# Fixed accumulator banks, a new order of the weights' splits, and expert 0's last chunk by column pairs, in an attention and mixture-of-experts kernel

## The chip, the cores and the metric

The kernel runs on one core of a Trainium2 chip. The time is the device time of one execution in microseconds; the median of several executions counts. Everything is computed in float32, where each matrix product is split into a high and a low part so that the tensor engine can take it in three passes.

## The reference

```python
attn = softmax(mask(q @ k.T / sqrt(64)))        # 8 batches, 8 heads, 576 positions, window of 64
x = (attn @ v) as rows [4608, 512]
noisy = x @ w_gate + log1p(exp(x @ w_noise)) * noise      # 8 experts
top2, weights = two best experts of each row, softmax over the two
for e in range(8):
    for k in range(2):
        m = top2[:, k] == e
        h = np.maximum(x[m] @ w1[e], 0.0)       # 512 -> 1024
        out[m] += weight[m] * (h @ w2[e])       # 1024 -> 512
```

## The kernel before, in words

**Stages.** Up to about 225 us the kernel computes attention and routes each row to two experts; the rows then lie in DRAM as xrows. After that it walks over a work list of chunks (e, c): expert 0 has three chunks (384, 384 and 448 rows), each of experts 1 to 7 has two (576 and 640 rows). A chunk is tiles of 128 rows, the 576 one with a fifth tile of 64.

**A chunk.** Its tokens are gathered and turned (transposed) ahead, beside the chunk before. Then PE runs the first layer (`up`) and the second (`down`).
- `gather` (L670): `whole` (L675, POOL) brings a tile's rows in by an indirect DMA into a buffer xg, of which there are four, which the outputs of the second layer use too. `turn_out` (L687) and four `turn_in` (L692), both on SP's queue, send them through DRAM so that they land as xc in blocks. `gate_of` (L679) copies the gate weight.
- `turn`: for each tile DVE transposes 32 x 32 blocks (`f`, L737, two instructions), then `g` makes the sums that the first layer's scheme wants and splits them into a high part xh (ACT, L749 and L755) and a low part xl (DVE, L751 and L756).
- `up`: for experts 1 to 7 the first layer is done by seven half-size products per group of columns g (0 to 3) in place of eight (L841 to L843 are the three passes). Product 2 opens a group in bank y, products 5 and 3 go to bank v, the others to a ring of three banks z. ACT copies (L867) or writes the relu (L853), DVE adds (L872) and makes the low part (L857). For expert 0 `up_first` runs the plain first layer, one column block f after the other.
- `down`: the second layer of a chunk by tiles. A tile takes 24 matmuls (16 for the 64-row tile), then ACT evicts it with the gate (L995; L997 and DVE's L998 and L999 for the 64-row tile) and POOL adds it into the output by an indirect DMA (`add_rows`, L917). The first tiles are interleaved with the first layer's last products.

**Banks.** `BANKS["d"]` is d0, d1 and y. `down` takes a tile's bank from the ring (L975), which runs on from chunk to chunk, so that every third tile is in y, also where the next chunk's first product opens in y.

**Weights.** `load_w2` (L218, SP) brings 2 MB of an expert's second weights into ws; `load_w1` (L214) the next expert's first weights into the same place. Each is split into a high part (ACT, L242) and a low part (DVE, L234, which `lag` puts one item later). The first weights also need POOL's sums of columns (L264): `split_w1` gives lists of items, for each column group g its `raw` parts, its `sums`, and its `mixed` parts, which are made of the sums. The second weights' load is issued when the last `mixed` part is read, since it goes to the same buffer.

**Order.** There is no scheduler: each engine takes its instructions as the program writes them. `spread(main, total, *parts)` (L77) runs the generator of matmuls and puts side work between its steps: a part (a, b, items) is laid out evenly from the fraction a to the fraction b of the `total` steps. The main loop (L1115 on) says where the gathers, the turn and the splits stand in the first and second layer of each chunk.

Of the kernel before, what the change touches and what calls it, by code (L numbers as in the profile page):

```python
# [22 lines left out]
KD, KF = DM // 128, F // 128  # L23
# [64 lines left out]
def tile_kernel(ctx, tc, qT, kT, vx, vT, wgx, noise, w1, w2, out):  # L88
# [115 lines left out]
    w2s = ws.rearrange("p (f d) -> p f d", f=KF)  # L204
# [5 lines left out]
    W2 = {}  # L210
# [17 lines left out]
    def lag(items, eng=nc.vector):  # L228
        todo = [None]

        def low_part():
            if todo[0]:
                x, h, l = todo[0]
                eng.tensor_tensor(l, x, h.bitcast(F32), op=OP.subtract)  # L234
            todo[0] = None

        def step(it):
            if callable(it):
                return lambda: (low_part(), it())

            def f():
                nc.scalar.activation(it[1], it[0], AF.Copy)  # L242
                low_part()
                todo[0] = it
            return f
        return [step(it) for it in items] + [low_part]

    def split_w1(ahead=False, add=nc.gpsimd, eng=nc.vector):
        def cols(g):
            return (w1s[:, :, x * 512 + g * 128:x * 512 + g * 128 + 128] for x in range(2))  # L250

        def parts(g, a, n, src):
            return (src, *(x.rearrange("p a k f -> p (a k) f")[:, 2 * a:2 * a + n, g * 128:g * 128 + 128]
                           for x in (WH, WL)))

        def raw(g):
            u, v = cols(g)
            return [parts(g, 0, 4, u), parts(g, 2, 2, v[:, 2:4])]

        def sums(g):  # L260
            u, v = cols(g)
            todo = ((v[:, 2:4], v[:, 0:2], v[:, 2:4], OP.add), (v[:, 0:2], v[:, 0:2], u[:, 0:2], OP.subtract),
                    (u[:, 0:2], v[:, 2:4], u[:, 0:2], OP.subtract), (u[:, 2:4], u[:, 2:4], u[:, 0:2], OP.subtract))
            return [lambda: [add.tensor_tensor(o, a, b, op=op) for o, a, b, op in todo]]  # L264

        def mixed(g):
            u, v = cols(g)
            return [parts(g, 5, 4, v), parts(g, 3, 4, u)]
        if ahead:
            return [lag([x for g in range(4) for x in raw(g) + sums(g)], eng), lag([x for g in range(4) for x in mixed(g)], eng)]  # L270
        a, b, c, d = (raw(0) + sums(0), raw(1) + sums(1) + mixed(0), raw(2) + sums(2) + mixed(1),
                      raw(3) + sums(3) + mixed(2) + mixed(3))
        return [lag(x, eng) for x in (a, b, c, d)]

    def split_w2():
        return lag([(w2s[:, f], W2["h"][:, f], W2["l"][:, f]) for f in range(KF)])


    VG = idle[:, 0:256].rearrange("p (n c) -> p n c", n=1)
# [494 lines left out]
    EXB, BANKS = {}, {}  # L774
# [8 lines left out]
    def up_first(c):  # L783
        e, n = 0, FIRST[c]
        main = n // 128 * 128
        tail = n - main
        HH[e, c] = [], [], []
        xh, xl = XH.pop((e, c)), XL.pop((e, c))
        for f in range(KF):
            if c == 0 and f < 4:  # L790
                hid = [x[:, f] for x in spare] + [None]
            else:
                if f == (0 if c else 4):
                    hb = EXB["p"].tile([128, 2, KF, 2 * HALF], F32R, name="hb")
                hid = [hb[:, 0, f, :384], hb[:, 1, f, :384],
                       hb[:, 0, f, 384:384 + 2 * tail].rearrange("p (s t) -> p s t", s=2) if tail else None]
            for a, b in zip(HH[e, c], hid):
                a.append(b)
            p = bank()
            fs = slice(f * 128, (f + 1) * 128)  # L800
            for k in range(KD):
                nc.tensor.matmul(p[:, :n], lhsT=w1h[:, k, fs], rhs=xh[:, k, :n], start=(k == 0), stop=False)
                nc.tensor.matmul(p[:, :n], lhsT=w1h[:, k, fs], rhs=xl[:, k, :n], start=False, stop=False)
                nc.tensor.matmul(p[:, :n], lhsT=w1l[:, k, fs], rhs=xh[:, k, :n], start=False, stop=(k == KD - 1))
                if k < KD - 1:
                    yield
            h, l, t = (x[f] for x in HH[e, c])
            nc.scalar.activation(h, p[:, :main], AF.Relu)
            nc.vector.scalar_tensor_tensor(l, p[:, :main], 0.0, h.bitcast(F32), op0=OP.max, op1=OP.subtract)
            if tail:  # L810
                nc.scalar.activation(t[:, 0], p[:, main:n], AF.Relu)
                nc.vector.scalar_tensor_tensor(t[:, 1], p[:, main:n], 0.0, t[:, 0].bitcast(F32),
                                               op0=OP.max, op1=OP.subtract)
            yield
# [3 lines left out]
    def ring(name):  # L818
        turns[name] += 1
        return BANKS[name][turns[name] % len(BANKS[name])]  # L820
# [135 lines left out]
    def down(e, c):  # L956
        if e == 0:
            yield from down_first(c)
            return
        wt = GW[e, c]  # L960
        hb = HH.pop((e, c))
        w2h, w2l = W2["h"], W2["l"]
        order = (0, 4, 1, 5, 2, 6, 3, 7)
        size = dict(tiles(e, c))
        steps = [(0, 0, 4), None, (0, 4, 6), (1, 0, 2), None, (1, 2, 6), (0, 6, 8), (1, 6, 8)]
        steps += [(q, 0, 8) for q in size if q > 1]
        P_ = {}
        for s in steps:
            if not s:
                yield from late.pop(0)  # L970
                continue
            q, i0, i1 = s
            m = size[q]
            if i0 == 0:
                P_[q] = ring("d")  # L975
            p = P_[q]
            for i in range(i0, i1):
                f = order[i]
                a, b = dict(start=(i == 0), stop=False), dict(start=False, stop=(i == KF - 1))
                if m == 128:  # L980
                    h, l = (hb[:, x, f, q * 128:q * 128 + 128] for x in range(2))
                    nc.tensor.matmul(p, lhsT=h, rhs=w2h[:, f, :], **a)  # L982
                    nc.tensor.matmul(p, lhsT=h, rhs=w2l[:, f, :], start=False, stop=False)  # L983
                    nc.tensor.matmul(p, lhsT=l, rhs=w2h[:, f, :], **b)  # L984
                else:
                    t = hb[:, 0, f, q * 128:q * 128 + 2 * m]
                    nc.tensor.matmul(p, lhsT=t, rhs=w2h[:, f, :], **a)
                    nc.tensor.matmul(p, lhsT=t, rhs=w2l[:, f, :], **b)
                if i < KF - 1:
                    yield  # L990
            if i1 < KF:
                continue
            y = exa.tile([128, XW], F32, name="xg", bufs=XB)[:, :DM]
            if m == 128:
                nc.scalar.activation(y, p, AF.Copy, scale=wt[:, q:q + 1])  # L995
            else:
                nc.scalar.activation(y[:m], p[m:2 * m], AF.Copy)  # L997
                nc.vector.tensor_tensor(y[:m], y[:m], p[:m], op=OP.add)  # L998
                nc.vector.tensor_scalar(y[:m], y[:m], wt[:m, q:q + 1], None, op0=OP.mult)  # L999
            add_rows(e, c, q, m, y)  # L1000
            yield
# [112 lines left out]
    for n, (e, c) in enumerate(work):  # L1114
# [3 lines left out]
        if n == 0:  # L1118
            for w in split_w2():
                side += [lambda: (drain(3), drain_slots(1))] * 2 + [w]  # L1120

            def catch_up():
                while (0, 1, 2) not in XG:
                    drain(1)
                    drain_slots(1)
        elif n == 1:
            pending.append(count())
            side += [lambda: (drain(6), drain_slots(1))] * 12
            side += [settle, lambda: drain_slots(10 ** 6), lambda: [x() for x in first_list(2)], lambda: None]
        elif c == 0:  # L1130
            parts.append((0.45, 0.95, split_w2()))
        if nxt and n:
            side += gather(*nxt) + [lambda: None] * 2
        if last and nxt:
            nextw = split_w1(e == 0)
            parts += [(0.55, 0.75, nextw[0]), (0.8, 1.0, nextw[1])] if e else [(0.1, 1.0, nextw[0])]
        parts.append((0.0, 1.0, side))
        if n == 0:
            parts.append((0.0, 0.8, [zero_out] * ZUP))
# [2 lines left out]
        total = KF * len(tiles(e, c)) + (4 if e else 0)  # L1142
        free = 12.5 / total
        if e == 0:
            parts = [(0.7, 1.0, side) if nxt[0] == 0 else (0.05, 0.9, side)]
            if last:
                parts.append((0.0, 0.8, nextw[1]))
        else:
            if c == 0:
                load_w1(e + 1)  # L1150
            parts = [(free, 0.86, side)]
            if last and nxt:
                parts.append((free, 0.9, nextw[2] + nextw[3]))
        if n == 1:
            load_w1(1)
            parts.append((0.0, 0.6, list(other_lists())))
# [125 lines left out]
```

## Time and profile before

| | |
|---|---|
| median of three executions | 1087.65 us (1087.3, 1087.65, 1090.16) |
| the profiled execution | 1086.88 us, span 1085.2 us |
| mean granted clock of TensorE | 0.969 |
| PE busy | 996.1 us, 92% |
| PE's weight loads busy | 888.8 us, 82% |
| DVE busy | 709.2 us, 65% |
| ACT busy | 521.6 us, 48% |
| POOL busy | 436.7 us, 40% |

The profiled execution is longer than its span by 1.7 us, which lie before and after what the profiler records. PE is the matrix engine, DVE the vector engine, ACT the scalar engine, POOL the general one, SP the engine that only issues DMAs here. A share is an average over stages; where PE stands still for another engine is seen only in the waits and the timelines.

### The profile page before, as it was taken

What the parts mean: (1) busy time and instruction counts of PE and PEld (TensorE: products, weight loads), DVE (VectorE), ACT (ScalarE), POOL (GpSimd) and SP (SyncE); (2) the same over time, 40 slices, a digit from 0 to 9 for tenths busy, and PEclk for the clock granted to TensorE, in tenths of its full rate; (3) what the DMA queues carried; (4) which work ended last, traced back from release to release, by engine and by line L of the source; (5) the groups of instructions that cost most, each with busy time, mean ns of one, the idle gap of its engine ahead of it and who ended that gap; (6) DMA issues with size and microseconds to landing.
All of it is one profiled execution on the core that took longest, in us unless ns stands there. A gap on an engine that the chain in (4) does not pass through costs nothing.

```text
span 1085.2 us, 22040 instructions
## 1 busy us (share of the span) xinstructions
PE 996.1 (92%) x8433; PEld 888.8 (82%) x8433; DVE 709.2 (65%) x1692; ACT 521.6 (48%) x1305; POOL 436.7 (40%) x577
## 2 busy tenths in 40 slices
PE   9887778879998999899989999998999998999995
PEld 8776777769787898889887979897989787978894
DVE  5688878583267667666776676668666756675630
ACT  4885665422245454535453445344544543554430
POOL 4436536332354154416432543255234614362202
PEclk9998997989998999999999999999999999999998
DMA  9987887783346653675267527653845485437303
GB/s 334 358 269 225 253 273 222 254 263 87 69 103 185 161 133 47 194 165 137 40 200 157 141 30 219 142 138 45 243 109 131 73 232 109 115 63 210 45 2 51
DMA packets 107235, 168.94 MB, mean 156 GB/s; under 512 B 13360, under 2 KB 57648, under 8 KB 105328
## 3 DMA queue, kind: packets, MB, share of 16 engines
q1 hardware_dynamic: 89968, 126.96, 38.2%
q0 software_dynamic: 17152, 40.48, 20.5%
q8 instruction: 68, 1.11, 0.4%
q14 instruction: 47, 0.39, 0.1%
HBM read 110.08 MB, written 57.32 MB: 154 GB/s over the span
## 4 chain that ended last, share of the span: by engine, by line
PE 56%; DVE 21%; DMA 9%; ACT 7%; issue 3%; POOL 3%; SPq 1%; POOLq 0%; DVEq 0%; ACTq 0%
PE ps_z L841 5%; PE ps_z L842 5%; PE ps_z L843 5%; PE ps_d L983 4%; PE ps_d L982 4%; PE ps_d L984 4%; PE ps_v L841 3%; PE ps_v L842 3%; PE ps_v L843 2%; PE ps_y L984 2%; PE ps_y L982 2%; PE ps_y L983 2%; DMA ws<-in_w_dram 2%; DVE xl L751 2%; DVE WL L234 2%
## 5 line engine op out<-in xcount | busy, mean ns | idle before, releaser
L917 POOL DMA_INDIRECT out_dram<-xg,los x70 | 114.7, 1638 | 264.9 <-ACT xg L995 232.9
L853 ACT ACTIVATE hb<-tq 128x288 fp32r<-128x288 f32 (+1 forms) x168 | 76.2, 459 | 147.8 <-DVE tq L872 147.5
L841 PE MATMUL ps_z<-xh,WH 128*128 128x288 f32 (+1 forms) x448 | 138.3, 309 | 0.0
L842 PE MATMUL ps_z<-xl,WH 128*128 128x288 f32 (+1 forms) x448 | 136.4, 305 | 0.0
L843 PE MATMUL ps_z<-xh,WL 128*128 128x288 f32 (+1 forms) x448 | 136.3, 304 | 0.0
L872 DVE TENSOR_TENSOR tq<-ps_z,tq 128x288 f32<-128x288 f32 (+1 forms) x168 | 78.3, 471 | 82.9 <-PE ps_z L843 82.2
L264 POOL TENSOR_TENSOR ws<-ws 128x256 f32<-128x256 f32 x112 | 94.4, 843 | 90.7 <-ACT WH L242 68.5
L983 PE MATMUL ps_d<-w2l,hb 128*128 128x512 f32 x328 | 127.8, 390 | 0.0
L982 PE MATMUL ps_d<-w2h,hb 128*128 128x512 f32 x328 | 127.8, 390 | 0.0
L984 PE MATMUL ps_d<-w2h,hb 128*128 128x512 f32 x328 | 127.7, 389 | 0.0
L857 DVE SCALAR_TENSOR_TENSOR hb<-tq,hb 128x320 fp32r<-128x320 f32 (+2 forms) x168 | 82.3, 493 | 41.0 <-ACT hb L853 37.2
L675 POOL DMA_INDIRECT xg<-xrows,lxs x70 | 72.9, 1041 | 84.9 <-DMA xs<-xg 33.1
L755 ACT ACTIVATE xh<-tq 128x512 fp32r<-128x512 f32 (+1 forms) x70 | 42.8, 611 | 101.1 <-DVE tq L753 101.1
L841 PEld LDWEIGHTS ps_z<-xh,WH 128*128 128x128 f32 x448 | 85.6, 191 | 2.8
L842 PEld LDWEIGHTS ps_z<-xl,WH 128*128 128x128 f32 x448 | 85.5, 191 | 1.1
L843 PEld LDWEIGHTS ps_z<-xh,WL 128*128 128x128 f32 x448 | 85.4, 191 | 0.0
L756 DVE TENSOR_TENSOR xl<-tq,xh 128x512 fp32r<-128x512 f32 (+1 forms) x70 | 46.6, 666 | 47.4 <-ACT xh L755 47.4
L234 DVE TENSOR_TENSOR WL<-ws,WH 128x512 fp32r<-128x512 f32 x112 | 74.7, 676 | 4.2 <-ACT WH L242 4.2
L841 PE MATMUL ps_v<-xh,WH 128*128 128x288 f32 (+1 forms) x224 | 70.7, 316 | 5.9 <-ACT tq L867 5.9
L341 POOL TENSOR_TENSOR t<-t,mx 128x512 f32<-128x512 f32 x36 | 38.0, 1055 | 93.7 <-DVE mx L340 73.1
L395 ACT ACTIVATE x<-ps_o,r 128x80 f32<-128x80 f32 x288 | 66.8, 347 | 14.4 <-DVE r L387 14.2
L984 PEld LDWEIGHTS ps_d<-w2h,hb 128*128 128x128 f32 x328 | 61.6, 188 | 13.0
(248 smaller groups left out, 2590.8 us busy)
## 6 DMA issues: line engine op xcount, KB each, us to landing
ws<-in_w_dram SPq DMA_DIRECT2D x14, 2048.0 KB, 10.3
xs<-xg SPq DMA_DIRECT2D x63, 256.0 KB, 3.5
vw<-in_vx_dram SPq DMA_DIRECT2D x36, 272.0 KB, 4.8
out_dram<-zero SPq DMA_DIRECT2D x38, 256.0 KB, 3.7
qc<-in_qT_dram SPq DMA_DIRECT2D x36, 256.0 KB, 5.0
KW<-in_kT_dram SPq DMA_DIRECT2D x36, 256.0 KB, 4.5
vt<-in_vT_dram SPq DMA_DIRECT2D x36, 256.0 KB, 4.2
xrows<-x SPq DMA_DIRECT2D x36, 256.0 KB, 4.4
```

The source lines that it names most:

```text
L234: eng.tensor_tensor(l, x, h.bitcast(F32), op=OP.subtract)
L264: return [lambda: [add.tensor_tensor(o, a, b, op=op) for o, a, b, op in todo]]
L841: nc.tensor.matmul(p[:, :n], lhsT=WH[:, a, k, w], rhs=xh[:, b, k, :n], start=first and k == 0, stop=False, **free)
L842: nc.tensor.matmul(p[:, :n], lhsT=WH[:, a, k, w], rhs=xl[:, b, k, :n], start=False, stop=False, **free)
L843: nc.tensor.matmul(p[:, :n], lhsT=WL[:, a, k, w], rhs=xh[:, b, k, :n], start=False, stop=(k == 1), **free)
L853: nc.scalar.activation(hh[:, f, a:b], src, AF.Relu)
L857: nc.vector.scalar_tensor_tensor(hl[:, f, a:m], src[:, :m - a], 0.0, hh[:, f, a:m].bitcast(F32), op0=OP.max, op1=OP.subtract)
L872: nc.vector.tensor_tensor(t, a[:, :n], t, op=OP.add)
L917: s = nc.gpsimd.indirect_dma_start(out=out[:(2 + seen.get((e, c), NT)) * 128], out_offset=bass.IndirectOffsetOnAxis(ap=LT[e, c][1][q][:m], ...
L982: nc.tensor.matmul(p, lhsT=h, rhs=w2h[:, f, :], **a)
L983: nc.tensor.matmul(p, lhsT=h, rhs=w2l[:, f, :], start=False, stop=False)
L984: nc.tensor.matmul(p, lhsT=l, rhs=w2h[:, f, :], **b)
```

## The change

Five edits:
1. `down` (experts 1 to 7): tile 0 has bank y, tiles 1 to 4 have d0, d1, d0, d1, in every chunk.
2. `split_w1`: the lists for the second layer of a last chunk. Before: raw(2), sums(2), mixed(1) and then raw(3), sums(3), mixed(2), mixed(3), one list behind the other. Now: raw(2), sums(2), raw(3), sums(3), mixed(1), mixed(2), mixed(3).
3. `split_w2` stands from 0.6 to 1.0 of a first chunk's first layer, where it stood from 0.45 to 0.95, and goes in the order in which `down` takes the blocks.
4. The turn's items end at 0.82 of the second layer (0.86 before), for expert 0 at 0.8 (0.9).
5. Expert 0's last chunk: `up_first` goes through its column blocks in the order 0, 4, 1, 5, 2, 6, 3, 7, and expert 1's first weights are split in eight lists, of which seven stand in the first layer and only mixed(3) in the second, up to 0.4 (before: one list of raw and sums in the first layer, one of all mixed in the second up to 0.8).

```diff
         if ahead:
-            return [lag([x for g in range(4) for x in raw(g) + sums(g)], eng), lag([x for g in range(4) for x in mixed(g)], eng)]
-        a, b, c, d = (raw(0) + sums(0), raw(1) + sums(1) + mixed(0), raw(2) + sums(2) + mixed(1),
-                      raw(3) + sums(3) + mixed(2) + mixed(3))
-        return [lag(x, eng) for x in (a, b, c, d)]
+            return [lag(raw(g) + sums(g), eng) for g in range(4)] + [lag(mixed(g), eng) for g in range(4)]
+        a, b, c = (raw(0) + sums(0), raw(1) + sums(1) + mixed(0),
+                   raw(2) + sums(2) + raw(3) + sums(3) + mixed(1) + mixed(2) + mixed(3))
+        return [lag(x, eng) for x in (a, b, c)]
 
     def split_w2():
-        return lag([(w2s[:, f], W2["h"][:, f], W2["l"][:, f]) for f in range(KF)])
+        return lag([(w2s[:, f], W2["h"][:, f], W2["l"][:, f]) for f in (0, 4, 1, 5, 2, 6, 3, 7)])
...
-        HH[e, c] = [], [], []
+        HH[e, c] = [None] * KF, [None] * KF, [None] * KF
...
-        for f in range(KF):
+        for f in (0, 4, 1, 5, 2, 6, 3, 7) if tail else range(KF):
...
-                a.append(b)
+                a[f] = b
...
             if i0 == 0:
-                P_[q] = ring("d")
+                P_[q] = BANKS["d"][2 if q == 0 else 1 - q % 2]
...
         elif c == 0:
-            parts.append((0.45, 0.95, split_w2()))
+            parts.append((0.6, 1.0, split_w2()))
...
             nextw = split_w1(e == 0)
-            parts += [(0.55, 0.75, nextw[0]), (0.8, 1.0, nextw[1])] if e else [(0.1, 1.0, nextw[0])]
+            parts += ([(0.55, 0.75, nextw[0]), (0.8, 1.0, nextw[1])] if e else
+                      [(a, b, nextw[q]) for q, a, b in ((0, 0.02, 0.12), (1, 0.14, 0.3), (2, 0.33, 0.5), (4, 0.34, 0.5),
+                                                       (3, 0.55, 0.75), (5, 0.56, 0.75), (6, 0.8, 1.0))])
...
         if e == 0:
-            parts = [(0.7, 1.0, side) if nxt[0] == 0 else (0.05, 0.9, side)]
+            parts = [(0.7, 1.0, side) if nxt[0] == 0 else (0.05, 0.8, side)]
             if last:
-                parts.append((0.0, 0.8, nextw[1]))
+                parts.append((0.0, 0.4, nextw[7]))
         else:
             if c == 0:
                 load_w1(e + 1)
-            parts = [(free, 0.86, side)]
+            parts = [(free, 0.82, side)]
             if last and nxt:
-                parts.append((free, 0.9, nextw[2] + nextw[3]))
+                parts.append((free, 0.9, nextw[2]))
```

The order on ACT at the end of expert 2's second layer, last chunk (L995 evicts an output tile, L242 makes a high part of weights, L749 and L755 copy turned tokens, L867 belongs to the next chunk's first layer). Before:

```order
L995 ACTIVATE xg<-ps_d_3967,wg 128x512
L242 ACTIVATE WH<-ws 128x4x128
L749 ACTIVATE xh<-tq 128x6x64
L755 ACTIVATE xh<-tq 128x8x64
L242 ACTIVATE WH<-ws 128x4x128 x2
L995 ACTIVATE xg<-ps_y_3972,wg 128x512
L749 ACTIVATE xh<-tq 128x6x32
L755 ACTIVATE xh<-tq 128x8x32
L242 ACTIVATE WH<-ws 128x4x128
L995 ACTIVATE xg<-ps_d_3966,wg 128x512
L867 ACTIVATE tq<-ps_y_3972 128x288
```

Now:

```order
L995 ACTIVATE xg<-ps_d_3967,wg 128x512
L242 ACTIVATE WH<-ws 128x4x128
L749 ACTIVATE xh<-tq 128x6x64
L755 ACTIVATE xh<-tq 128x8x64
L242 ACTIVATE WH<-ws 128x4x128 x3
L749 ACTIVATE xh<-tq 128x6x32
L755 ACTIVATE xh<-tq 128x8x32
L995 ACTIVATE xg<-ps_d_3966,wg 128x512
L242 ACTIVATE WH<-ws 128x4x128
L995 ACTIVATE xg<-ps_d_3967,wg 128x512
L867 ACTIVATE tq<-ps_y_3972 128x288
```

The last tile of the turn (the two copies of 32 columns) has moved ahead of the fourth tile's eviction, and neither of the last two evictions reads the bank that L867 reads.

POOL in the first layer of expert 0's last chunk (L264 are the column sums, L675 the gathers for expert 1, L679 the gate weights). Before:

```order
L675 DMA xg<-xrows,lxs 128x528 x4
L264 TENSOR_TENSOR ws<-ws 128x2x128 x4
L679 COPY wg<-xg 128x1
L675 DMA xg<-xrows,lxs 64x528
L264 TENSOR_TENSOR ws<-ws 128x2x128 x4
L679 COPY wg<-xg 128x1 x2
L264 TENSOR_TENSOR ws<-ws 128x2x128 x4
```

Now:

```order
L675 DMA xg<-xrows,lxs 128x528 x2
L264 TENSOR_TENSOR ws<-ws 128x2x128 x4
L675 DMA xg<-xrows,lxs 128x528 x2
L264 TENSOR_TENSOR ws<-ws 128x2x128 x4
L679 COPY wg<-xg 128x1
L675 DMA xg<-xrows,lxs 64x528
L264 TENSOR_TENSOR ws<-ws 128x2x128 x4
```

Two groups of sums now stand ahead of the fifth gather, where one did.

## Rows read from the trace of the kernel before

**Rows 1.** PE's waits, 225 us to the end (what waited <- releaser: total us, times, longest)
```profile
PE ps_y L841 <- ACT xh L749: 9.8, 5, 4.7
PE ps_y L841 <- ACT xg L995: 7.7, 2, 3.8
```

**Rows 2.** timeline of PE: first-layer products (start us, length us, [idle before, releaser])
```profile
334.89 0.61 PE L841 MATMUL ps_y<-xh,WH 128*128 128x288 f32 x1 [4.75 <-ACT xh L749]
...
441.05 0.40 PE L841 MATMUL ps_y<-xh,WH 128*128 128x288 f32 x1 [3.83 <-ACT xg L995]
...
490.66 0.30 PE L841 MATMUL ps_y<-xh,WH 128*128 128x320 f32 x1
...
559.72 0.40 PE L841 MATMUL ps_v<-xh,WH 128*128 128x288 f32 x1 [1.56 <-ACT tq L867]
...
597.46 0.41 PE L841 MATMUL ps_y<-xh,WH 128*128 128x320 f32 x1 [1.54 <-DVE xg L998]
...
915.20 0.42 PE L841 MATMUL ps_y<-xh,WH 128*128 128x320 f32 x1 [2.75 <-DVE xg L998]
```

**Rows 3.** windows of six us from such starts (length, PE busy, granted clock, DMA share, GB/s)
```profile
440.00:446.00 6.00, 4.95 (x25) 0.72 0.89 205
...
597.00:603.00 6.00, 5.54 (x37) 1.00 0.35 58
```

**Rows 4.** timeline of SP's queue: loads of second weights (L218) and first turn_in (L692)
```profile
334.11 0.35 SPq L218 DMA_DIRECT2D ws<-in_w_dram  x1
...
355.21 0.32 SPq L692 DMA_DIRECT2D xc<-xs  x1
...
441.59 0.35 SPq L218 DMA_DIRECT2D ws<-in_w_dram  x1
...
463.27 0.32 SPq L692 DMA_DIRECT2D xc<-xs  x1
...
547.26 0.35 SPq L218 DMA_DIRECT2D ws<-in_w_dram  x1
...
654.05 0.35 SPq L218 DMA_DIRECT2D ws<-in_w_dram  x1
...
758.26 0.35 SPq L218 DMA_DIRECT2D ws<-in_w_dram  x1
...
777.95 0.32 SPq L692 DMA_DIRECT2D xc<-xs  x1
...
863.90 0.35 SPq L218 DMA_DIRECT2D ws<-in_w_dram  x1
...
973.33 0.35 SPq L218 DMA_DIRECT2D ws<-in_w_dram  x1
```

**Rows 5.** timeline of DVE: first transposes of tiles in the turn (L737)
```profile
315.59 0.45 DVE L737 STREAM_TRANSPOSE tq<-xc 128x256 f32<-128x256 f32 x1 [3.77 <-DMA xc<-xs]
...
320.18 0.44 DVE L737 STREAM_TRANSPOSE tq<-xc 128x256 f32<-128x256 f32 x1
...
472.28 0.45 DVE L737 STREAM_TRANSPOSE tq<-xc 128x256 f32<-128x256 f32 x1 [0.48 <-DMA xc<-xs]
...
577.12 0.45 DVE L737 STREAM_TRANSPOSE tq<-xc 128x256 f32<-128x256 f32 x1 [0.22 <-DVE hb L857]
...
788.38 0.43 DVE L737 STREAM_TRANSPOSE tq<-xc 128x256 f32<-128x256 f32 x1
...
895.14 0.45 DVE L737 STREAM_TRANSPOSE tq<-xc 128x256 f32<-128x256 f32 x1 [1.70 <-DMA xc<-xs]
...
899.01 0.45 DVE L737 STREAM_TRANSPOSE tq<-xc 128x256 f32<-128x256 f32 x1
```

**Rows 6.** timeline of POOL: a group of sums (L264), and expert 0's last whole scatter-add
```profile
297.69 3.51 POOL L264 TENSOR_TENSOR ws<-ws 128x256 f32<-128x256 f32 x4 [0.88 <-ACT WH L242]
...
333.56 1.91 POOL L917 DMA_INDIRECT out_dram<-xg,lo  x1 [6.55 <-ACT xg L941]
```

**Rows 7.** DMA issues: the loads of whole weights (KB each, median us to landing)
```profile
ws<-in_w_dram SPq DMA_DIRECT2D x14, 2048.0 KB, 10.3
```

## The prediction

> **What bounds the kernel now.** Read the table of PE's waits from 225 us on first: in the expert part only a few rows count. The product that opens a chunk (bank y, L841) waited five times for the turned tokens, 9.8 us, and twice for an eviction, 7.7 us [rows 1]. Then go to PE's timeline for their places [rows 2]: 4.75 us at 334.89 (expert 1), 3.83 at 441.05 (expert 2; expert 5 has its like), 1.54 at 597.46 and 2.75 at 915.20 (second chunks of experts 3 and 6, on DVE's eviction of a 64-row tile). The other four waits for tokens are (9.8 - 4.75) / 4 = 1.26 each. A fourth kind stands inside a first layer: 1.56 at 559.72, a product whose bank waits for an ACT copy that stands behind the split of the second weights; experts 3, 6 and 7 have it.
>
> A wait can cost more than itself. The windows [rows 3] show PE's granted clock at 0.72 in the six microseconds after the wait of 3.83, and after that of 2.75 alike, which is part 2.4 GHz and part 1.2 GHz: 6 x 0.28 = 1.68 us of work lost. After the wait of 1.54 it stayed 1.00. After the waits of 1.26 it fell once in four.
>
> But PE's waits are the end of a loop, and the queues show what closes it. SP issues the load of an expert's second weights (L218) as soon as DVE has split the last of the first weights. Only afterwards do the last scatter-adds and the gathers for the next chunk get through, and SP's first turn_in (L692) follows 463.27 - 441.59 = 21.68 us after the load in expert 2 [rows 4]. The tokens land 9.0 us later, and DVE starts to turn them at 472.28 [rows 5], 30.69 after the load. From there to the next load it is 547.26 - 472.28 = 74.98 us: five tiles turned, a first and a second layer, the next turn, the next split. Loops last 105.67 (441.59 to 547.26), 106.79 (to 654.05) and, the longest, 109.43 (863.90 to 973.33). I read this as a chain: load, scatter-add, gather, turn, first layer, second layer, split, load. In expert 2 the turn starts 0.48 us after DVE went idle for these tokens, so there the chain holds, although PE idled 3.83 at the chunk before. That idle time was cover.
>
> **The change, part by part.** The sum is made against the profiled execution, 1086.88 us (span 1085.2), 0.77 below the median of 1087.65.
>
> *Fixed banks.* Tile 0 goes to y and the last tile to a d bank. So y is free when the next chunk opens, and the waits on evictions (3.83 twice, 1.54, 2.75) have no cause left. What it is worth depends on the chain. Expert 2's and expert 5's 3.83 lie ahead of a chain that was late anyway: removed, the same time appears at the second chunk, where turned tokens are needed. The arithmetic: the last tile's first copy ends 4 x 3.87 (895.14 to 899.01 [rows 5]) + two transposes of 0.45 + 0.5 = 16.9 after the turn starts, thus 30.7 + 16.9 = 47.6 after the load. PE opened that chunk at 490.66 [rows 2] without a wait, 49.1 after the load, and without the 3.83 and the 1.68 that followed it would come at 43.6. So 4 us of waiting return there, and I count nothing for expert 2 on this account. Expert 3's 1.54 and expert 6's 2.75 lie after the turn, on the path: turn to load took 76.93 in expert 3 (577.12 to 654.05) and 78.19 in expert 6 (895.14 to 973.33) against 74.98, so 1.95 and 3.21 go.
>
> *Two banks where three ran on.* Tile 4 now needs tile 2's eviction. Tile 3 covers it; a few tenths at most, under the chain: 0.
>
> *Turn earlier (0.82), fewer mixed splits in front.* In the second layer one split on DVE (the 0.72 by which a tile with splits, 4.59, is longer than one without, 3.87; both below) fewer stands before the third tile. The turn of the next first chunk, for which PE waits 1.26, comes 0.4 earlier (0 to 0.7). In six loops: -2.4 (-4.2 to 0).
>
> *Second weights split later.* They leave the place where the ACT copy waited behind them; 1.56 goes in experts 3, 6 and 7, but in front of the late tokens, so it is cover like expert 2's. One thing remains: in expert 5 the turn at 788.38 began 10.43 after its turn_in (777.95), where 9.01 would do (463.27 to 472.28); earlier work on DVE held it. 1.42 goes, and 0.54 of its 75.52 to the load: -1.96.
>
> Gains: expert 1, 2 and 4 nothing but the 0.4 each; 3: 1.95; 5: 1.96; 6: 3.21; and 2.4: **-9.5**.
>
> *What it costs.* In the second layer of a last chunk the eviction of the fourth tile (L995) now stands on ACT behind the turn's last copy (L755); before it stood ahead of that tile's two copies, as the order shown with the change has it. Its scatter-add is therefore issued just as the load starts, and moves its 256 KB beside the load's 2048 KB, which take 10.3 us [rows 7]. The nearest row is expert 1's: a whole tile's scatter-add was issued at 333.56 [rows 6], the load at 334.11, the turn_in at 355.21, 21.10 after it, against 21.68 in expert 2 and 19.69 in expert 5 (758.26 to 777.95), mean 20.69 [rows 4]. I take +0.4 in six loops, **+2.4**. Lower bound 0, since the gathers wait for buffers either way; upper 1.3 a loop, an eighth of 10.3.
>
> The Trainium skill, "DMA: Bandwidth & Descriptors", Queues, rings and completion order, says that each engine takes turns between the queues that have work for it, packet by packet. By it the load would be stretched by all of the scatter-add's bytes, an estimate of 1.3 us a loop, and the forecast would read 5.4 us later; expert 1's row shows less.
>
> *Half clock at second chunks.* PE will wait there now, 4 us in expert 2, about as long in 6, and near none to 2 in the others. By the windows a wait of 2.75 or more costs 1.68; I take two of the six: **+3.4** (0 to 8.4). The half clock of expert 2 and 5 after the eviction falls away, but lies in the cover.
>
> *Expert 0's last chunk.* Its groups' sums and mixed splits move into the first layer, so the second layer has one list left instead of two. On POOL one more group of sums, four operations of together 3.51 us [rows 6], stands before the last gather, which had 0.88 us idle ahead of it: tokens 2.6 later than 315.59, where DVE waited 3.77 for them [rows 5]. In return, the turn has fewer splits between its tiles: 3.87 a tile where none stands there, for the 4.59 from 315.59 to 320.18, three tiles long: -2.2. Net **+0.4** (-2.2 to +2.6).
>
> Sum: -9.5 + 2.4 + 3.4 + 0.4 = -3.3, thus 1083.6 for the profiled execution and **1084.3** for the median, 0.3% less. With the bounds the case has a range of 1078 to 1091.
>
> **Rivals.** *The waits simply vanish.* If the chain is looser than I read it (the gathers' time shrinks when PE runs earlier, because scatter-adds and buffers come earlier as well), all that PE waits is gained: 7.7 + 1.54 + 2.75 of evictions, 3 x 1.56 before products, about 2.5 of the waits for tokens, 3 x 1.68 of half clock: 24 us, 1063.4. For it: nothing in rows 4 says that 21.68 could not shrink (in expert 5 it is 19.69). Against it: nothing in the change moves the gathers ahead of the load, and with 30.69 after every load DVE stood waiting. 0.18.
>
> *Slower: the scatter-add in the load's shadow.* The eviction behind the turn puts the fourth tile's scatter-add beside the load in every loop; the gather that reuses its buffer waits for it, and 1.3 us a loop go into the chain, 6 x 1.3 = 7.8. PE then waits at second chunks by enough for the half clock in five loops, 8.4. -9.5 + 7.8 + 8.4 + 0.4 = +7.1: **1094.8**. It decides from 0.9 us a loop with four half clocks (5.4 + 6.7 + 0.4 > 9.5 + 3). For it: the order on ACT is plain, and the half clock follows each long wait. Against it: 21.10 in expert 1. 0.24.
>
> *It does nothing:* the gains are cover throughout and costs small. This lies inside my own case, whose range holds both signs.
>
> **Chances.** My case 0.58, vanish 0.18, slower 0.24. Some 0.3% (3.3 us) is what a measurement of this kernel can tell from no change: 1084.4 to 1090.9. My forecast lies on that border: of its 0.58, 0.26 falls below, 0.31 inside, 0.01 above. Faster 0.44, same 0.31, slower 0.25. The range reaches to 1070 and 1095, which leaves out most of the first rival and the worse half of the second, some 0.2.
>
> **What would show it.** Right: no wait of a y product for an eviction in the waits; waits of 1 to 4 us on xh or xl at second chunks (about 486 and 806); load to turn still 29 to 31 us; turn to load 74.5 to 75 in all loops; no wait near 560. The first rival: load to turn falls to 27 or less. The second: turn_in 22 or more after the load, and granted clock 0.72 after five second chunks' openings. I am wrong if PE still waits on y, if loops differ by over 2 us, or if expert 1 starts later than 337.

## The result, and the profile after

The changed kernel takes 1099.61 us in the median of eight executions (1093.98 to 1109.98), the kernel before 1087.71 (1086.43 to 1090.35) beside it: ratio 1.0106, 95% interval 1.0066 to 1.0147. It is slower by some 1.1%, where I had forecast 0.3% less, and it lies beyond my range. In these eight executions it also spreads four times as far, 16.0 us against 3.9; that this belongs to the change is not shown, since the kernel before spread over 14.2 us in 29 later executions.

The profiled execution took 1101.77 us (span 1100.0). Waits of PE from 225 us on, what waited <- releaser, total, times, longest (answers to [rows 1]):

```profile
PE ps_y L841 <- ACT xh L749: 11.6, 7, 5.1
PE ps_d L982 <- ACT xg L995: 5.7, 6, 1.6
...
PE ps_d L987 <- ACT xg L995: 2.7, 3, 1.1
```

The waits of a chunk's first product for an eviction are gone, as the change means it, and so are the waits of v products near 560. New are waits on ps_d: tile 4 for tile 2's eviction, and nothing of the kind stood in the table before. The waits for tokens went from five to seven, and moved: before, they stood at first chunks; now, but for expert 1's, at second ones, where PE's timeline has, for the second chunk of expert 2:

```profile
497.78 0.41 PE L841 MATMUL ps_y<-xh,WH 128*128 128x320 f32 x1 [1.46 <-ACT xh L749]
```

Half speed follows. Windows (length, PE busy, granted clock, DMA share, GB/s) behind the openings of the second chunks of experts 2, 3, 4 and 6, as against [rows 3]:

```profile
498.00:506.00 8.00, 7.54 (x28) 0.58 0.25 33
608.00:614.00 6.00, 6.00 (x30) 0.72 0.36 46
714.00:720.00 6.00, 5.84 (x28) 0.72 0.30 40
929.00:935.00 6.00, 5.77 (x29) 0.72 0.34 44
```

Four of seven, each with a part of the stretch at 1.2 GHz; I had counted two. The first costs 8 x 0.42 = 3.4 us, the others 1.7 each, together 8.4. The trace before has four such stretches as well, at other places (from 441, 653, 759 and 916 on, granted clock 0.72 over six us each, together 6.7). In sum that is 1.7 us more than before.

The queue of SP shows where the time went. Load of the second weights (L218) and first turn_in (L692), experts 2, 3 and 6, as against [rows 4]:

```profile
448.35 0.35 SPq L218 DMA_DIRECT2D ws<-in_w_dram  x1
...
471.88 0.32 SPq L692 DMA_DIRECT2D xc<-xs  x1
...
558.47 0.35 SPq L218 DMA_DIRECT2D ws<-in_w_dram  x1
...
579.89 0.32 SPq L692 DMA_DIRECT2D xc<-xs  x1
...
877.41 0.35 SPq L218 DMA_DIRECT2D ws<-in_w_dram  x1
...
900.96 0.32 SPq L692 DMA_DIRECT2D xc<-xs  x1
```

From load to turn_in it is 23.53, 21.42 and 23.55 us. Over experts 2 to 7 the mean is 22.48; in the trace before it was 20.78. DVE, at the first tile of the turn, waits as the end of this (answers to [rows 5]):

```profile
480.90 0.77 DVE L737 STREAM_TRANSPOSE tq<-xc 128x256 f32<-128x256 f32 x2 [4.98 <-DMA xc<-xs]
```

**Where the 14.8 us of the two spans lie.** Up to the start of expert 1's second turn 5.90, of which 3.74 stand already at 225 us, in code that the change does not touch (that stage ended between 225.5 and 234.0 in the 14 traces of this study, whatever the kernel). From that turn to expert 2's load 0.86. In the five loops from expert 2's load to expert 7's 6.23: 5.48 from load to turn, 0.75 from turn to load. Behind the last load 1.81. The medians differ by 11.9; without the 3.74 the traces differ by 11.1.

Laid against the forecast: from load to turn, experts 2 to 7, I had +1.0 (2.4 less expert 5's 1.42), and it is 5.48 and 1.81, thus +7.3. It would be 10.2 by turn_in alone (6 x 1.7), but in experts 5 and 6 the turn now starts 1.4 and 1.3 us sooner after its turn_in. From turn to load I had -4.7, and it is +0.75. Some 3 us more stand ahead of expert 2's load; they were not taken apart.

So the chain got longer on the side where I had put +0.4 a loop, and the side where I had put most of the gains gave nothing in sum.

### The profile page after: what moved, and what is told of

It reads as the page before. It is cut to its first block, busy times and chain, and to the rows that moved or that the text cites. A ratio compares the mean times of both kernels' runs of the same rounds, so it can differ in the third digit from the quotient of the medians.

```text
span 1100.0 us, 22046 instructions
## 1 busy us (share of the span) xinstructions
PE 1010.9 (92%) x8433; PEld 891.9 (81%) x8433; DVE 713.7 (65%) x1692; ACT 521.5 (47%) x1305; POOL 434.4 (39%) x577
## 4 chain that ended last, share of the span: by engine, by line
PE 37%; DVE 24%; DMA 13%; issue 10%; ACT 7%; POOL 5%; SPq 1%; DVEq 0%; POOLq 0%; ACTq 0%
DMA xc<-xs 5%; DMA xg<-xrows,lxs 4%; DVE tq L737 3%; PE ps_z L841 3%; PE ps_z L843 3%; PE ps_z L842 3%; DMA xs<-xg 3%; DVE xl L756 3%; DVE xl L751 3%; ACT xh L755 3%; PE ps_o L376 2%; POOL ws L264 2%; PE ps_d L984 2%; PE ps_d L983 2%; POOL out_dram L917 2%
## 5 line engine op out<-in xcount | busy, mean ns | idle before, releaser
L917 POOL DMA_INDIRECT out_dram<-xg,los x70 | 110.6, 1580 | 298.7 <-ACT xg L995 264.2
L982 PE MATMUL ps_d<-w2h,hb 128*128 128x512 f32 x392 | 153.3, 391 | 5.7 <-ACT xg L995 5.7
L983 PE MATMUL ps_d<-w2l,hb 128*128 128x512 f32 x392 | 152.7, 390 | 0.0
L984 PE MATMUL ps_d<-w2h,hb 128*128 128x512 f32 x392 | 152.5, 389 | 0.0
L264 POOL TENSOR_TENSOR ws<-ws 128x256 f32<-128x256 f32 x112 | 98.4, 878 | 69.5 <-ACT WH L242 62.2
L675 POOL DMA_INDIRECT xg<-xrows,lxs x70 | 71.9, 1027 | 88.3 <-DMA xs<-xg 38.3
L982 PEld LDWEIGHTS ps_d<-w2h,hb 128*128 128x128 f32 x392 | 73.6, 188 | 23.0 <-ACT xg L995 8.3
L755 ACT ACTIVATE xh<-tq 128x512 fp32r<-128x512 f32 (+1 forms) x70 | 42.7, 611 | 102.6 <-DVE tq L753 102.6
L984 PEld LDWEIGHTS ps_d<-w2h,hb 128*128 128x128 f32 x392 | 73.6, 188 | 15.5
L983 PEld LDWEIGHTS ps_d<-w2l,hb 128*128 128x128 f32 x392 | 73.6, 188 | 14.6
L234 DVE TENSOR_TENSOR WL<-ws,WH 128x512 fp32r<-128x512 f32 (+1 forms) x112 | 77.5, 702 | 4.6 <-ACT WH L242 3.2
L749 ACT ACTIVATE xh<-tq 128x384 fp32r<-128x384 f32 (+1 forms) x70 | 35.6, 508 | 89.5 <-DVE tq L737 88.2
```

The costliest lines, as they stand in the source:

```text
L917: s = nc.gpsimd.indirect_dma_start(out=out[:(2 + seen.get((e, c), NT)) * 128], out_offset=bass.IndirectOffsetOnAxis(ap=LT[e, c][1][q][:m], ...
```

## The theory and its rival

POOL's timeline around expert 3's load (558.47), where L917 are scatter-adds and L675 gathers:

```profile
557.47 1.64 POOL L917 DMA_INDIRECT out_dram<-xg,los  x1 [6.23 <-ACT xg L995]
...
559.41 1.55 POOL L917 DMA_INDIRECT out_dram<-xg,los  x1 [0.27 <-issue]
561.27 1.02 POOL L675 DMA_INDIRECT xg<-xrows,lxs  x1 [0.30 <-issue]
562.60 0.97 POOL L675 DMA_INDIRECT xg<-xrows,lxs  x1 [0.30 <-issue]
568.67 0.94 POOL L675 DMA_INDIRECT xg<-xrows,lxs  x1 [5.10 <-DMA out_dram<-xg,los]
569.97 1.19 POOL L675 DMA_INDIRECT xg<-xrows,lxs  x1 [0.36 <-issue]
...
573.97 0.98 POOL L675 DMA_INDIRECT xg<-xrows,lxs  x1 [2.52 <-DMA xs<-xg]
```

And what POOL waited for at 557.47, on ACT:

```profile
556.20 0.42 ACT L755 ACTIVATE xh<-tq 128x256 fp32r<-128x256 f32 x1 [1.07 <-DVE tq L753]
556.52 0.67 ACT L995 ACTIVATE xg<-ps_d,wg 128x512 f32<-128x512 f32 x1
```

The fourth tile's eviction stands behind the turn's last copy, so its scatter-add is issued 1.0 us before the load; the fifth tile's is issued 0.9 after it. Now two of the four buffers are held by scatter-adds beside the load. Only two gathers get through; the third waits for the first scatter-add until 10.2 us after the load, and the fifth is issued 15.5 after it (mean of experts 2 to 7: 16.5; before, 14.2). The fourth came only 0.9 us later in the mean (11.6 for 10.7). The fifth waits for the first turn_out, which frees its buffer, and that transfer takes longer: where a trace has its landing, 2.0 to 2.1 us in the kernel before (three loops), and 4.1 to 4.3 in the kernel before with the turn to 0.82 (three loops), whose run stands below. That it is the third gather, now beside it, that slows it was not tried.

**Theory B:** this late scatter-add alone makes the loss, and the waits of PE on ps_d lie in its cover (time that would be lost there anyway). **Theory A:** it and the waits for two banks together. **Theory C:** the two banks alone.

## The experiments

All ratios are against the kernel before, run beside each on the same chip; its own median was 1091.05 to 1091.84 us in these runs, so the ratios are to be compared and not the microseconds. The expectations were written against 1087.7 us; where a time is compared with them, it is given on that scale too (the ratio times 1087.7). "Load to turn_in" is the mean over experts 2 to 7 of the SP timeline of the profiled execution.

| kernel | ratio, 95% interval | load to turn_in, us |
|---|---|---|
| the change | 1.0106, 1.0066 to 1.0147 | 22.48 |
| the change, three banks | 1.0143, 1.0112 to 1.0173 | 22.39 |
| the change, turn to 0.85 | 1.0123, 1.0073 to 1.0172 | 23.07 |
| the change, turn to 0.86 | 0.9955, 0.9932 to 0.9977 | 21.05 |
| three banks, turn to 0.86 | 0.9942, 0.9920 to 0.9964 | 20.58 |
| three banks, turn to 0.90 | 0.9967, 0.9941 to 0.9992 | 20.29 |
| three banks, 0.86, expert 0 as before | 0.9926, 0.9895 to 0.9956 | 21.21 |
| three banks, 0.86, second weights in halves | 1.0024, 0.9999 to 1.0049 | 22.43 |
| the change without that scatter-add | 0.9887, 0.9853 to 0.9920 | 19.72 |
| before, turn to 0.82 | 1.0111, 1.0069 to 1.0152 | 22.60 |
| before, three banks | 0.9955, 0.9931 to 0.9980 | 20.90 |
| before, the change's banks | 0.9960, 0.9933 to 0.9986 | 20.64 |
| before, second weights later | 1.0006, 0.9977 to 1.0034 | 20.62 |

### Undo one part: the turn's end, the banks, both

```diff
-            parts = [(free, 0.82, side)]
+            parts = [(free, 0.86, side)]
```

> The changed kernel with the turn of experts 1 to 7 ending at 0.86 of the second layer again (0.82 in the change), so that the fourth tile's eviction stands on ACT ahead of the turn's last two copies; two d banks as in the change. Theory A: first turn_in 20 to 21.5 us after the load (22.5 on average in the changed kernel), waits at second chunks' openings below 1 us and half clock there in at most two; the ps_d waits stay: 1087 to 1093. Theory B: 1084 to 1089. Theory C: no change within 3 us, 1097 to 1102.

1085.97 us, ratio 0.9955, or 1082.8 on the expectations' scale: a little below theory B's 1084 to 1089 and well below A's 1087 to 1093; C is out. The one number makes a kernel that is slower by 1.1% into one that is faster than the kernel before. POOL around expert 3's load (553.10), and the eviction on ACT:

```profile
549.68 1.85 POOL L917 DMA_INDIRECT out_dram<-xg,los  x1 [3.67 <-ACT xg L995]
...
552.78 1.72 POOL L917 DMA_INDIRECT out_dram<-xg,los  x1 [1.22 <-ACT xg L995]
554.81 1.27 POOL L675 DMA_INDIRECT xg<-xrows,lxs  x1 [0.31 <-issue]
556.38 0.97 POOL L675 DMA_INDIRECT xg<-xrows,lxs  x1 [0.30 <-issue]
557.65 0.95 POOL L675 DMA_INDIRECT xg<-xrows,lxs  x1 [0.30 <-issue]
564.23 0.95 POOL L675 DMA_INDIRECT xg<-xrows,lxs  x1 [5.63 <-DMA out_dram<-xg,los]
...
567.47 0.98 POOL L675 DMA_INDIRECT xg<-xrows,lxs  x1 [1.92 <-DMA xs<-xg]
```

```profile
548.73 0.67 ACT L995 ACTIVATE xg<-ps_d,wg 128x512 f32<-128x512 f32 x1
549.56 0.36 ACT L749 ACTIVATE xh<-tq 128x192 fp32r<-128x192 f32 x1 [0.16 <-DVE tq L737]
551.00 0.42 ACT L755 ACTIVATE xh<-tq 128x256 fp32r<-128x256 f32 x1 [1.07 <-DVE tq L753]
```

The eviction is ahead of the copies, the fourth scatter-add 3.4 us before the load, three gathers go at once, and the fifth is issued 14.4 after the load. Half clock at second chunks' openings fell from four to two.

```diff
-                P_[q] = BANKS["d"][2 if q == 0 else 1 - q % 2]
+                P_[q] = BANKS["d"][(2, 0, 1)[q % 3]]
```

> The changed kernel (1099.6 us) with the tiles on three fixed banks, y, d0, d1, y, d0 for tiles 0 to 4, in place of y, d0, d1, d0, d1; all else as changed. Theory A (two causes: the wait of tile 4 for tile 2's eviction, 0.8 to 1.6 us at the second layers in the trace of the changed kernel, 11.5 us by its longer second layers; and the late scatter-add beside the load): the waits on ps_d for an eviction go, second layers take 28.8 and 26.8 us again, but the first turn_in still comes 22 us or more after the load and second chunks still open after a wait on xh: 1088 to 1093. Theory B (only the late scatter-add in the loop counts, the bank waits lie in its cover): the waits on ps_d go, and the same time appears as waits at the second chunks' openings: 1097 to 1100. Theory C (only the bank waits count): 1086 to 1088 and no long waits at second chunks.

1106.24 us, ratio 1.0143, or 1103.3 on the expectations' scale: not faster than the change, and above what all three theories expected. Second layers take 26.8 and 28.8 us again, but now tile 3 sits in y, its eviction is the late one, and the next chunk's product waits 3.2 us for it: the price moved from tile 4 to the chunk's opening. Three banks gave nothing here, where the eviction itself is late.

Both edits together:

> Both edits of the two runs before together: three fixed banks and the turn to 0.86. Theory A: both causes gone, what is left of the change is its gains: first layers of first chunks 22.7 us in all experts, no wait at the opening of first chunks but 1.3 us for xh: 1076 to 1084, faster than the kernel before (1087.7). Theory B: 1084 to 1089, the same as with the turn at 0.86 alone. Theory C: 1086 to 1088, as with three banks alone.

1083.52 us, ratio 0.9942, or 1081.4 on the expectations' scale. As a number this lies in theory A's 1076 to 1084 and below B's 1084 to 1089. What tells the two apart is the step from the run before: A had some 10 us between the two runs, B none. The ratios, 0.9955 and 0.9942, differ by 1.4 us, and their intervals overlap. So B holds as far as is measured: once the scatter-add is early, a third bank makes no difference clear of the noise; a gain of up to some 5 us is not excluded. From turn to load the five loops now take 74.84, 74.72, 74.74, 74.80 and 74.75: this is the figure that I had forecast for the change.

### One part alone: the turn's end in the kernel before

```diff
-            parts = [(free, 0.86, side)]
+            parts = [(free, 0.82, side)]
```

> The kernel before (1087.7 us; banks, splits and expert 0 as before) with nothing but the turn of experts 1 to 7 ending at 0.82 of the second layer, where it ended at 0.86. On ACT the fourth tile's eviction of a last chunk then stands behind the turn's last two copies, as in the change. If that alone makes the change slow: the fourth tile's scatter-add is issued within 1.5 us of the load, the fourth gather waits for the scatter-add before it, the fifth is issued 16 to 17 us after the load (14.2 before), the first turn_in 22 to 23.5 after it (20.8), and the time is 1095 to 1104. If it takes the new banks or the new split order as well: 1085 to 1091.

1102.24 us, ratio 1.0111, or 1099.8 on the expectations' scale: the whole loss of the change, with none of its other parts. The fourth tile's scatter-add goes out 1.0 us before expert 3's load (549.74), and POOL shows the same picture:

```profile
548.75 1.73 POOL L917 DMA_INDIRECT out_dram<-xg,los  x1 [4.49 <-ACT xg L995]
...
559.62 0.95 POOL L675 DMA_INDIRECT xg<-xrows,lxs  x1 [4.67 <-DMA out_dram<-xg,los]
...
566.30 0.98 POOL L675 DMA_INDIRECT xg<-xrows,lxs  x1 [3.77 <-DMA xs<-xg]
```

Here it is the third gather that waits, and the fifth comes 16.6 us after the load. New banks or split orders are not needed for it.

### Order or amount: 0.85

```diff
-            parts = [(free, 0.82, side)]
+            parts = [(free, 0.85, side)]
```

> The changed kernel with the turn ending at 0.85 (0.82 in the change; 0.86 gave a ratio of 0.9955). On ACT this differs from 0.86 in one place of each last chunk: the fourth tile's eviction still stands behind the turn's last two copies. If the order of eviction and copies decides: a step, 1095 to 1103 and first turn_in 22 us or more after the load. If the amount by which the turn is earlier decides, by a proportion of 0.82 to 0.86: 1085 to 1092.

1103.02 us, ratio 1.0123 against 0.9955 at 0.86: a step, and no proportion. The order of DVE and POOL is the same at 0.85 and 0.86. On ACT the expectation says too little: not only in last chunks but in first chunks too the turn's last copies move ahead of the fourth tile's eviction, and in each last chunk one copy of weights (L242) moves as well. These places together are worth 1.7%; that it is the one in last chunks follows from the run without that scatter-add, below. The half clock does not make this step: this slow kernel has four stretches of it between 350 and 1060 us, as many as the kernel before. The other side was tried too, 0.90 with three banks:

> Three fixed banks and the turn ending at 0.90 (0.86 gave a ratio of 0.994). The fourth tile's eviction stands ahead of the copies as at 0.86. By the order: within 4 us of 0.86, and the first chunks open later by more waiting for xh (1.0 us at 0.86, 1.5 to 3 here) with load to turn_in still 20 to 21 us: 1083 to 1090. If a later turn were better by itself: under 1081.

Ratio 0.9967, not told apart from 0.86. The eviction stands ahead of the turn's last copies as at 0.86; the wait for xh ahead of first chunks grew from 1.0 to 1.8 us, and load to turn_in is 20.29 (20.58 at 0.86).

### Take the suspect away

```diff
-            add_rows(e, c, q, m, y)
+            if q != 3 or c == 0:
+                add_rows(e, c, q, m, y)
```

> The changed kernel (1099.6 us) without the scatter-add of the fourth tile of each expert's last chunk (experts 1 to 7): those rows are not added to the output. The turn still ends at 0.82, the order on ACT and the two d banks are those of the change. If the scatter-add beside the load is what costs (the gathers wait for its buffer): three gathers are issued within 5 us of the load as in the kernel before, first turn_in 19.5 to 21.5 after it, 1083 to 1090. If it is the place of the eviction on ACT or the turn's place by another way: 1096 to 1102, with turn_in at 22 or more.

This kernel leaves the fourth tile of each last chunk out of the output. 1080.68 us, ratio 0.9887, or 1075.4 on the expectations' scale, better than expected: turn_in 19.72 after the load. The order on ACT, in first chunks too, is that of the change, and so are the two banks, whose waits make the last chunks' second layers as long as in the change (some 30 us for 28.8). So neither is what makes the change slower than the kernel before. It is the transfer beside the load that costs, not ACT's order in itself. This kernel also saves the transfer's bytes and POOL's time, so its ratio is not the price of the order alone.

### The other parts of the change

```diff
-                P_[q] = ring("d")
+                P_[q] = BANKS["d"][2 if q == 0 else 1 - q % 2]
```

> The kernel before with nothing but the change's banks (y, d0, d1, d0, d1). My price of these two banks was 0 for tile 4's wait for tile 2's eviction, and the gain at expert 3 and 6 about 5 us less what comes back: 1082 to 1086, ratio 0.995 to 0.999, tile 4's wait under 0.3 us. If the 1.1 us longer second layers of the changed kernel come from the two banks alone and count: 1088 to 1096.

Ratio 0.9960, 1085.22 us, or 1083.4 on the expectations' scale: as costed. All waits of y for evictions are gone, no ps_d wait appears among PE's waits, and some of the gain comes back as waits inside first layers. Three banks alone, `(2, 0, 1)[q % 3]`:

> The kernel before (1087.7 us) with nothing but the three fixed banks y, d0, d1, y, d0. The waits of a chunk's first product for an eviction (3.83 twice, 1.54, 2.75) go. If the loop through load, gather and turn sets the period as I read it, expert 2's and 5's 3.83 come back as waits at the second chunks and only experts 3 and 6 gain: 1082 to 1086. If the waits were simply lost time, with their half clock: 1072 to 1077. If nothing but cover: 1087 to 1089.

0.9955, the same. The simple reading, that the 24 us of waits and half clock are lost time to be had, is out in both.

```diff
-            parts.append((0.45, 0.95, split_w2()))
+            parts.append((0.6, 1.0, split_w2()))
```

with the blocks in the order 0, 4, 1, 5, 2, 6, 3, 7:

> The kernel before with nothing but the second weights' split at 0.6 to 1.0 in the new order. I counted the 1.56 us waits of experts 3, 6 and 7 as cover and 1.96 us in expert 5 as gain: the waits of v products for an ACT copy go, first layers of first chunks take 22.6 us everywhere, and the time is 1084 to 1088 (ratio 0.997 to 1.000). If those waits were lost time: 1080 to 1083.

Ratio 1.0006, just above the 0.997 to 1.000 that I expected: the waits near 560 were cover. The first layers of experts 3 and 6 fell from 24.6 to 22.45 us, and PE's waits ahead of their second chunks grew from 1.54 and 2.75 us to 2.27 and 4.39.

Expert 0's part undone (part 5 of the change and the 0.8 for its turn), in the kernel with three banks and 0.86:

> Three fixed banks and the turn at 0.86 (1083.5 us, ratio 0.994) with expert 0's part as in the kernel before: column blocks in order, one list of raw parts and sums, one of mixed parts up to 0.8, the turn to 0.9. If that part of the change is about neutral, as I costed it (+0.4, -2.2 to +2.6): 1081 to 1086, expert 1 opens within 2.5 us of its time, and its load comes some 9 us later but the turn after it at the same time. If it is worth something: 1086 to 1090.

Ratio 0.9926 against 0.9942 with that part: not told apart, so about neutral, as costed. Expert 1 opens 44.9 us after the mark at which expert 0's last chunk opens, and 45.9 with the part. Without the part its load comes 10.6 us later against the chunk's opening, and the next turn only 1.0 us later.

### An attempt at more: the load in halves

```diff
-            load_w2(e + 1)
+            load_w2(e + 1, slice(0, 2))
+            load_w2(e + 1, slice(4, 6))
...
+            if e and c == 0:
+                side[5:5] = [lambda: load_w2(e, slice(2, 4)), lambda: load_w2(e, slice(6, 8))]
```

> Three fixed banks and the turn at 0.86 (1083.5 us, ratio 0.994), and the second weights loaded in halves: blocks 0, 1, 4, 5 at once, blocks 2, 3, 6, 7 from SP's queue behind the first turn_out. If the loop is load, scatter-add, gather, turn_in: with 1 MB ahead of them the last scatter-add lands sooner, the fourth gather comes 7 to 8 us after the load (10.8), the turn starts 27 to 28.5 us after the load (29.8), waits at second chunks vanish, and the time is 1076 to 1082. If the queue's bytes in all set it: no change, 1082 to 1086. If the late half holds up the split of the second weights: waits on w2h in second layers, 1086 to 1095.

A miss: ratio 1.0024, or 1090.3 on the expectations' scale. The fourth gather came earlier, as hoped (9.2 us after the load in expert 3, where it is 11.1 in the kernel with 0.86 alone), and the fifth 12.1 to 14.6. But the second half then lies ahead of four of the five turn_outs, and the turn_in came at 22.43. The late half also held up the split of the second weights: ACT waited six times for it, 5.7 us in all, and PE's v products three times for ACT, 3.7 us in all, in first layers, where I had named second layers. How the loss is shared between the two was not tried; the bytes ahead of turn_in seem to count too, and not only the buffer's release.

## Why the prediction was wrong

**The chain was right.** Load, scatter-add, gather, turn, layers, split, load is the loop in all 14 traces, turn to load 74.7 to 78.6 us, and its first part goes with the time: the five changed kernels whose load to turn_in is 22.39 us or more in the mean have ratios of 1.0024 to 1.0143, the eight others (19.7 to 21.2) 0.9887 to 1.0006. PE's waits were cover where I called them so: the banks alone gave 0.4%, the second weights' split nothing.

**The step that failed** is "What it costs": the fourth tile's scatter-add at +0.4 a loop. The mechanism was named; the size was off. In experts 2 to 7 the turn_in came 1.7 us later (22.48 against 20.78), above the upper bound of 1.3. The row was badly chosen. In every loop of experts 2 to 7 of the trace before, one scatter-add stands beside the load, the last tile's, 0.3 us ahead of it; the change makes it two. About expert 1's load there are two already, but the second is that of expert 0's 64-row tile and goes out 4.09 us after the load, so that all gathers stand behind it and the third waits only 1.64 us for its buffer:

```profile
338.20 1.44 POOL L917 DMA_INDIRECT out_dram<-xg,lo  x1 [2.70 <-DVE xg L952]
...
343.88 0.94 POOL L675 DMA_INDIRECT xg<-xrows,lxs  x1 [1.64 <-DMA out_dram<-xg,lo]
```

The wait was to be seen in the loops of experts 2 to 7: POOL's fourth gather waits 5.72 us for the one scatter-add there, so a second one could hold the third gather about as long (it did, 5.10). How much of that reaches turn_in, 1.7 us, that row alone does not say:

```profile
546.94 1.72 POOL L917 DMA_INDIRECT out_dram<-xg,los  x1 [1.21 <-ACT xg L995]
...
551.82 0.95 POOL L675 DMA_INDIRECT xg<-xrows,lxs  x1 [0.31 <-issue]
558.49 0.95 POOL L675 DMA_INDIRECT xg<-xrows,lxs  x1 [5.72 <-DMA out_dram<-xg,los]
```

(the last scatter-add, the third and the fourth gather around the load at 547.26). The bound by bytes (an eighth of 10.3) left out the wait for a buffer.

**What follows from it** was mis-sized with it. I took two stretches of half clock at second chunks (+3.4); there were four, one of 3.4 us, together 8.4. They followed PE's waits of 0.4 to 1.5 us there, where I had foreseen waits of some 4 us in experts 2 and 6 and counted on half clock from 2.75 us on. The gains from turn to load (1.95, 0.54 and 3.21 in experts 3, 5 and 6) came as 0.46, 0.47 and 1.70, and experts 2 and 4 lost 2.59 and 0.79. In the kernel with three banks and 0.86 the five loops take 74.7 to 74.9, so with the scatter-add early the gain that I had costed is there.

**The slower rival** had the mechanism, place and size nearly right: 1.3 a loop and half clock in five of the openings, 1094.8; measured 1.7, four, 1099.6. It was given 0.24, since I held one row of expert 1 against it. My own range was also narrower than its terms: the bounds of the case, added up straight, run from 1074 to 1099, where I wrote 1078 to 1091.

**Two banks at 0** is open for the change itself: PE's waits on ps_d are 8.4 us there, where I said a few tenths. In the run without the scatter-add they stay (0.8 to 1.7 in six loops), and that kernel is faster than the kernel before; so they do not make the loss. With the turn at 0.86 they fall to 0.3 each at most second chunks and cost nothing that is measured. Tile 2's eviction stands on ACT behind a copy that waits 3.11 us for DVE:

```profile
547.65 0.63 ACT L755 ACTIVATE xh<-tq 128x512 fp32r<-128x512 f32 x1 [3.11 <-DVE tq L753]
...
548.71 0.67 ACT L995 ACTIVATE xg<-ps_d,wg 128x512 f32<-128x512 f32 x1
```

**The other terms held:** no wait for y on an eviction, none near 560, expert 0's part about neutral. Expert 1 opened at 339.87, beyond my 337, but 4.18 of the 4.98 stand at the opening of expert 0's last chunk.

The Trainium skill, "DMA: Bandwidth & Descriptors", Queues, rings and completion order, lets engines take turns between queues; by the estimate from it the load would be stretched by 1.3 us a loop. The measured 1.7 lies nearer to it than my 0.4, but the traces show another way: gathers that wait for a buffer. The load itself is not stretched: with two late scatter-adds (the kernel before, turn to 0.82) it landed 9.0 to 9.5 us after its issue in experts 2 to 7, with one (the kernel before) 9.1 to 10.3 in the three loops for which the trace has it.

**The better kernel.** The change with its turn ending at 0.86 and three fixed banks is faster than both: 0.9942 (0.9920 to 0.9964) of the kernel before, some 0.6%. With two banks and 0.86 it is 0.9955, without expert 0's part 0.9926; these three are not told apart.

## What to carry to other kernels

Where an engine's order is written by fractions, look at what each shift moves past what: here the place of an eviction on ACT, ahead of a copy that waits or behind it, decided 1.7% by a step. A store that must free a buffer was better off ahead of the bulk load that follows it; count how many buffers such stores hold at that moment, and look at the gather that already waits for one of them. When PE's waits are the end of a loop through queues, cost a change at the loop's link, and expect removed waits to return.

## What the runs showed that I had not expected

A scatter-add of one tile, from issue to landing, has a median of 4.9 us in the view of DMA issues of the kernel before:

```profile
out_dram<-xg,los POOLq DMA_INDIRECT x70, 4.9
```

Beside the load of 2 MB it holds its buffer about twice as long: issued at 557.47, it let the third gather go at 568.67, some 11 us later; the one at 552.78 in the kernel with 0.86 let the fourth go at 564.23, 11.4 later. Half clock at openings did not follow the time from kernel to kernel: 8.4 us of it in the change, 6.7 in the kernel before, and in the slow kernel with 0.85 as many stretches as in the kernel before.
